# Attention and two MLP layers on one Trainium2 core: batches cut into halves of 256 queries, the first block in single precision

## The chip, the cores and the metric

One core of one Trainium2 chip runs the whole kernel. The metric is device microseconds of one execution; lower is better. TensorE (PE) multiplies, VectorE (DVE) and ScalarE (ACT) do the elementwise work and empty PSUM, GpSimd (POOL) helps where PSUM is not read, SyncE (SP) issues the DMAs.

## The reference

Three stages follow one another. Single precision comes in and goes out; the MLP weights come in double precision.

```python
# attention: batch 4, heads 8, seq 576, head_dim 64
scores = scale * np.matmul(q, k.transpose(0, 1, 3, 2))
thresh = np.max(scores, axis=-1, keepdims=True) - tau
scores = np.where(scores >= thresh, scores, -1000000000.0)
attn = np.exp(scores - np.max(scores, axis=-1, keepdims=True))
attn = attn / (np.sum(attn, axis=-1, keepdims=True) + 1e-09)
x = np.matmul(attn, v)            # -> (2304 tokens, 512)
# layer 1: 512 -> 2048 -> 512
r = np.maximum(x @ w_in, 0.0)
x = (s * (r * r) + b) @ w_out
# layer 2: 512 -> 2048 -> 512
h = x @ w_in2
out = (h * (1.0 / (1.0 + np.exp(-1.702 * h)))) @ w_out2
```

The mask is sharp (only scores within tau of the row's maximum count), so the scores are computed in single precision or better. The rest keeps that precision by splitting a number into two f16 parts, high and low, and adding three products instead of one.

## The kernel before

**A plan, not a loop.** The class `Plan` collects steps (`add`): engines with an estimated cost, what is read and written, and a due time `prio`. `run` goes through the plan once with these costs and, on each engine, always starts the ready step with the smallest due time; the order that comes out is emitted as it stands, so each engine's queue is fixed before the run. `KN` holds the due times (in us) and buffer counts. A tile pool with `bufs` buffers gives them out in the order in which the steps were added.

**Attention** goes by pairs of heads, 4 for each of 4 batches, with 9 tiles of 128 queries a pair (`attention`, `tile_step`): PE computes 128 x 576 scores into two PSUM banks (L525 for batches 0 and 1, two single-precision products of 64 rows; L518 for batches 2 and 3, from operands split before), DVE finds the negative maximum `nm` (L539), then the threshold `tb` (L544) and the exponential's bias `nb` (L550), ACT takes the exponential (L557), DVE masks and sums (L561). ACT then writes an f16 copy `p16` (L335), POOL its low part (L570, L571), and a transposing DMA on SP's queue turns both into `PT` (L573). Scores have two buffers `S`; every third of the first 53 tiles goes to a third buffer `Sx`. After a pair's last tile its sums are inverted and turned by TensorE (L608, L612), the values are multiplied in f16 in 14 terms (`finish_main`, L633; the last 64 queries in `finish_last`, L661), and the result is scaled and split into `xs`, the operand of layer 1. `scan_v` finds the largest value of each head first, since V is scaled before it is split (`prep_v`).

**Weights.** Each of layer 1's 32 weight rows (512 KB of doubles) is loaded, turned into single precision by a cast on ACT or DVE (L745) and a DVE step (L749, `convert`); each group of four rows gets a norm (`norm`: PE products L783, DVE, PE L791, DVE) and is split into f16 parts (`split_w`, L827).

**Layer 1** goes by units of 256 queries: two for each batch and a ninth for the last 64 queries of all four. A unit needs `xs` of its whole batch. Its first half is 8 pairs of 128 hidden columns (`pair`, L901, 24 f16 matmuls a pair into one PSUM bank; ACT's L908 and L909 empty it), its second half two banks (`bank`, L929). One PSUM bank (`y`) serves pairs, banks and norms until `widen` turns the two banks of `Sx` into two more (`yy`); `widen` waits for the last tile in `Sx`.

**Layer 2** (L1054, L1099) follows in blocks of 512 tokens.

PSUM's eight banks: `S` 4, `Sx` 2 (later `yy` 2), `T` 1 (turned sums, values), `y` 1.

## Time and profile before

| | |
|---|---|
| median of 3 runs | 1074.03 us (1072.44 to 1074.36) |
| the profiled execution | 1071.84 us, span 1069.7 us |
| mean granted TensorE clock | 0.943 of full speed |
| PE busy | 976.5 us (91%), 7193 matmuls |
| DVE busy | 648.8 us (61%) |
| ACT busy | 580.6 us (54%) |
| POOL busy | 259.8 us (24%) |
| DMA | 121.88 MB, mean 114 GB/s |

The profile shows one execution. A span runs from the first instruction to the last; the profiled time has 2.1 us around it. Busy shares are averages over stages that differ, so the slices and stretches are read before the averages. The granted clock is TensorE's, as a share of 2.4 GHz; it has two levels, 1.2 and 2.4 GHz, and a share between them is a mix.

### The profile page before, as it was taken

To read this page: it belongs to the slowest core of one execution; us is meant where nothing else is said; L and a number is where in the kernel's file an instruction comes from. 1 tells how busy PE (TensorE), PEld (TensorE's weight loads), DVE (VectorE), ACT (ScalarE), POOL (GpSimd) and SP (SyncE) were. 2 spreads that over 40 slices of the span, in tenths; PEclk is the share of its full clock that TensorE was granted. 3 is DMA by queue.
4 is the path that set the end of the run, shared out by engine and by line. 5 is a ranking of instruction groups with operands and counts; after the bars stand their busy time and mean duration, and the time that the engine had idled before them with its cause. 6 is when DMAs were issued, how large, how long until landed. Compare 5 with 4: busy or idle time off the path is not lost.

```text
span 1069.7 us, 19065 instructions
## 1 busy us (share of the span) xinstructions
PE 976.5 (91%) x7193; PEld 652.5 (61%) x7193; DVE 648.8 (61%) x1517; ACT 580.6 (54%) x996; POOL 259.8 (24%) x359
## 2 busy tenths in 40 slices
PE   4665667879999999999999999999999999999998
PEld 2332234547888988888888888844444444444653
DVE  7989988887876788778534367486343333223210
ACT  5676676676675777776544567374332323323311
POOL 3554443333455666455400000000000000000000
PEclk7686567979999999999999999999999999999999
DMA  8899989856678687868632356201001001000001
GB/s 230 199 200 233 248 244 212 231 116 128 133 151 143 141 174 166 166 134 155 106 99 63 116 186 225 73 1 40 20 11 59 10 10 30 21 10 10 21 1 40
DMA packets 208636, 121.88 MB, mean 114 GB/s; under 512 B 178264, under 2 KB 183456, under 8 KB 208544
## 3 DMA queue, kind: packets, MB, share of 16 engines
q1 hardware_dynamic: 208544, 120.66, 47.4%
q8 instruction: 57, 0.93, 0.4%
q14 instruction: 35, 0.29, 0.1%
HBM read 68.16 MB, written 10.00 MB: 73 GB/s over the span
## 4 chain that ended last, share of the span: by engine, by line
PE 66%; DVE 2%; ACT 1%; issue 0%; ACTq 0%; DVEq 0%
PE S L1099 17%; PE yy L1054 12%; PE yy L929 10%; PE yy L901 7%; PE y L1054 6%; PE y L901 4%; PE y L929 4%; PE S L518 3%; PE T L633 2%; PE T L661 0%; ACT e L557 0%; DVE nm L539 0%; DVE l L827 0%; ACT gt L952 0%; DVE e L561 0%
## 5 line engine op out<-in xcount | busy, mean ns | idle before, releaser
L901 PEld LDWEIGHTS <-wb 128*128 128x128 f16 x1728 | 167.7, 99 | 28.4 <-issue 6.7
L929 PEld LDWEIGHTS <-wb 128*128 128x128 f16 x1728 | 168.5, 98 | 25.6 <-issue 3.8
L570 POOL TENSOR_TENSOR p<-e,p 128x512 f16<-128x512 f32 x112 | 134.3, 1199 | 200.5 <-ACT p L335 168.8
L1054 PEld LDWEIGHTS <-l 128*128 128x128 f16 x960 | 93.9, 98 | 92.7 <-issue 0.2
L929 PE MATMUL yy<-g,wb 128*128 128x256 f16 x1248 | 144.2, 275 | 1.7 <-ACT gt L952 0.9
L1054 PE MATMUL yy<-xs,l 128*128 128x512 f16 (+1 forms) x636 | 128.4, 357 | 0.0
L557 ACT ACTIVATE e<-S,nb 128x576 f32<-128x576 f32 x127 | 92.0, 734 | 40.7 <-DVE tb L544 18.5
L561 DVE SCALAR_TENSOR_TENSOR e<-S,tb,e 128x576 f32<-128x576 f32 x127 | 101.7, 810 | 20.4 <-ACT e L557 19.4
L901 PE MATMUL yy<-xs,wb 128*128 128x256 f16 x960 | 113.0, 273 | 0.0
L539 DVE TENSOR_REDUCE nm<-S 128x1 f32<-128x576 f32 x127 | 93.6, 749 | 31.2 <-PE S L518 17.6
L1099 PE MATMUL S<-wb,g 128*128 128x512 f16 x480 | 106.7, 379 | 0.0
L901 PE MATMUL y<-xs,wb 128*128 128x256 f16 x768 | 92.6, 277 | 3.8 <-DVE n L793 1.9
L335 ACT ACTIVATE p<-e 128x576 f16<-128x576 f32 x112 | 75.5, 677 | 35.9 <-DVE e L561 14.5
L1066 DVE SCALAR_TENSOR_TENSOR gt<-gt,yy 128x512 f32<-128x512 f32 (+1 forms) x53 | 33.3, 632 | 91.9 <-ACT gt L1062 91.9
L1099 PE MATMUL S<-wb,lg 128*128 128x512 f16 x384 | 85.5, 379 | 0.0
L1099 PEld LDWEIGHTS <-g 128*128 128x128 f16 x480 | 47.0, 98 | 55.7
L337 ACT ACTIVATE gt<-S,x2y 128x512 f32<-128x512 f32 x17 | 11.7, 688 | 112.6 <-PE S L1099 112.6
L525 PE MATMUL S<-kk,qa 64*128 64x288 f32 (+1 forms) x136 | 34.3, 599 | 37.5 <-DVE e L561 15.4
L1054 PE MATMUL y<-xs,l 128*128 128x512 f16 (+1 forms) x324 | 67.9, 359 | 0.0
L1099 PEld LDWEIGHTS <-lg 128*128 128x128 f16 x384 | 37.6, 98 | 45.1
L331 DVE CAST g<-gt 128x512 f16<-128x512 f32 x43 | 21.5, 501 | 60.6 <-ACT gt L909 60.5
L1066 DVE SCALAR_TENSOR_TENSOR gt<-gt,y 128x512 f32<-128x512 f32 (+1 forms) x27 | 17.2, 637 | 63.3 <-ACT gt L1062 63.3
(171 smaller groups left out, 1461.2 us busy)
## 6 DMA issues: line engine op xcount, KB each, us to landing
wst<-in_moe_w_in SPq DMA_DIRECT2D x32, 512.0 KB, 4.1
wst<-in_moe_w_out SPq DMA_DIRECT2D x32, 512.0 KB, 4.3
rv<-in_v SPq DMA_DIRECT2D x29, 320.0 KB, 3.2
raw<-in_k SPq DMA_DIRECT2D x16, 288.0 KB, 3.4
raw<-in_q SPq DMA_DIRECT2D x16, 288.0 KB, 3.2
yd<-gt SPq DMA_DIRECT2D x18, 256.0 KB, 2.3
l<-yd SPq DMA_DIRECT2D x16, 256.0 KB, 4.4
out<-gt SPq DMA_DIRECT2D x16, 256.0 KB, 2.0
```

Of the source, the lines that this page charges most:

```text
L335: nc.scalar.activation(dst(), src(), AF.Copy)
L518: nc.tensor.matmul(Sp[:, half, :HALF], q[h][j][:, qcols[h]], k[h][:, half * HALF : (half + 1) * HALF], start=(h, j) == (heads[0][0], 0), s ...
L525: nc.tensor.matmul(Sp[to, half, :HALF], q[h][r, qcols[h]], k[r, h * HALF : (h + 1) * HALF])
L539: {"DVE": 668.0}, lambda _: nc.vector.tensor_reduce(nm.ap, Sv(), AX.XY, ALU.max, negate=True), [Sp], [nm],
L557: lambda _: nc.scalar.activation(ev(), Sv(), AF.Exp, bias=nb.ap, scale=1.0), [Sp, nb], [e],
L561: lambda _: nc.vector.scalar_tensor_tensor(ev(), Sv(), tb.ap, ev(), ALU.is_ge, ALU.mult, accum_out=p["acc"][:, i, 0:1]),
L570: nc.gpsimd.tensor_tensor(p16[:, S + H2 :], e[:, :MAIN], p16[:, :MAIN], ALU.subtract)
L901: nc.tensor.matmul(hps[:, h, :], W[:, i, j, kk * P : (kk + 1) * P], x[:, k, kk, cols], start=t == 0, stop=t == len(terms) - 1,)
L929: nc.tensor.matmul(yp[:, h, :], self.W[0, 1, c][:, i, j, i0 * P : (i0 + 1) * P], u["g"][c][:, k, j, :], start=t == 0, stop=t == len(terms) ...
L1054: nc.tensor.matmul(hps[:, :n], W[:, i, j, kk * P : (kk + 1) * P], x[:, k, kk, :], start=t == 0, stop=t == 11)
L1066: lambda _: nc.vector.scalar_tensor_tensor(gt[:, :n], gt[:, :n], 1.0, hps[:, :n], ALU.add, ALU.mult),
L1099: nc.tensor.matmul(yp(), blk["g"][f // 2][:, k, f % 2, cols], self.W[1, 1, f // CH][:, w, f % CH, :], start=n == 0, stop=n == 47,)
```

## The change

Each batch's first 512 queries are worked in two halves of 256 (`heads`): for batches 0 and 1 all four pairs of heads do the first half (4 tiles a pair), then all four the second half with the last 64 queries (5 tiles); for batches 2 and 3 each pair does both halves in turn and keeps K and Q. Layer 1's units now need only their own half (`x_of`).

Batch 0 is worked in single precision (`fa` 2 halves): the masked exponential is turned by TensorE, five turns a tile into a two-bank buffer `TP`, and copied to `PT` by ACT; V is used as it was loaded, in 5 terms instead of 14. The bias is the maximum itself, and `tb` is computed on POOL. No f16 copy, low part or transposing DMA is left for these tiles. The value maxima of batch 0 are taken along the way.

The first unit of layer 1 is worked in single precision too (`fu` 1; `pair32`, `bank32`): 4 products for each 128 hidden columns instead of 12, with weights that are converted but neither normed nor split. The norms and splits of the first weights come during this unit's pairs (`split_in`), those of the second weights after it.

The two banks that `Sx` had go to `TP` first, then (`swap`) to a third scores buffer for every third tile of batches 1 and 2 (`sx` 24 pairs), then (`widen`, due at 300) to `yy`. Only steps that use `yy` wait for `widen` now (`gate`). Attention's PE steps get due times 300 us earlier than those of the other engines (`first`). Due times are set anew; `g` buffers are no longer lent to attention; `xs` has 4 buffers of half the size, `rv` 2 and `V` 4 buffers. `bank` is cut into four steps a half instead of two, and layer 2's `xs` into two buffers.

```diff
-    "lend": 6, "lp": 3, "lV": 1, "boost": 29.63, "mix": 14, "a0": 0, "p0": 20.89, "a1": 78.55, "p1": 28.98, "a2":
-    166.74, "p2": 0.72, "a3": 221.7, "p3": 0.72, "u0": 85.49, "du": 55.73, "win": 6.56, "wout": 60.47, "cpace":
-    4.0, "w2": 436.49, "c2pace": 7.19, "t2": 622.67, "d2": 126.93, "c0": 3, "tw": 2, "cast": 1, "g": 6, "wb": 9,
-    "xs": 2, "gt": 3, "lg": 6, "l8": 5, "scan": 0, "sx": 53.0, "wide": 0.45, "x2": 39.35, "y2": 0.99, "wf": 0,
-    "wm": 1, "wl": 1, "wv": 1, "wq": 1, "nm": 1, "tb": 22.97, "sc": 0, "eb": 3, "pb": 2, "pt0": 2, "pt1": 1, "rv":
-    1, "V": 1, "parts": 8, "raw": 1, "spread": 8,
+    "first": 300.0, "lend": 0, "lp": 3, "lV": 1, "boost": 0, "mix": 14, "a0": 0, "p0": 12.0, "a1": 110.0, "p1":
+    13.0, "a2": 230.0, "p2": 32.0, "a3": 360.0, "p3": 32.0, "u0": 60.0, "d0": 28.0, "opace": 2.0, "du": 44.0,
+    "win": 2.0, "wout": 55.0, "cpace": 3.4, "w2": 360.0, "c2pace": 5.0, "t2": 622.67, "d2": 126.93, "c0": 3, "tw":
+    2, "cast": 1, "g": 6, "wb": 9, "xs": 4, "gt": 3, "lg": 6, "l8": 5, "scan": 2, "fu": 1, "fa": 2, "half": 2,
+    "a0b": 50.0, "p0b": 14.0, "a1b": 165.0, "p1b": 14.0, "si": 110.0, "sp": 7.0, "so": 150.0, "sop": 5.0, "vs0":
+    300.0, "tbp": 1, "nbs": 1, "rvk": 1, "wide": 300.0, "sx": 24, "x2": 39.35, "y2": 0.99, "wf": 0, "wm": 1, "wl":
+    2, "wv": 3, "wq": 1, "nm": 1, "tb": 22.97, "sc": 0, "eb": 3, "pb": 2, "pt0": 2, "pt1": 1, "rv": 2, "V": 4,
+    "parts": 8, "raw": 1, "spread": 8,
...
-        op["prio"] = self.prio if prio is None else prio
+        op["prio"] = (self.prio if prio is None else prio) - self.first * ("PE" in engines)
...
+        if p["first"]:
+            p["k"], p["q"] = p["first"]["k"], p["first"]["q"]
+            return
...
+        if not p["f32"] and (b, hp) in self.kept:
+            p["v"] = self.kept[b, hp]
+            return
+        rv = self.at("rv", [P, 2, KS * D], F32, KN["rv"])
         self.load(lambda: rv.ap, lambda: self.v[b, hp], [rv], P * 2 * KS * D * 4)
-        V = self.at("V", [P, 2, 2 * KS, D], F16, KN["V"], KN["lV"])
-        p["v"] = V
+        if p["f32"]:
+            p["v"] = rv
+            if p["unit"] % 2 == 0:
+                self.most(b, hp, rv)
+            return
+        V = self.at("V", [P, 2, 2 * KS, D], F16, KN["V"])
+        p["v"] = self.kept[b, hp] = V
         part = lambda i: V.ap.rearrange("p h (i x) d -> p h i (x d)", i=2)[:, :, i]
...
         k, q = p["k"], p["q"]
-        Sp = self.ps("S", [P, 2, 512], (p["b"] * NP + p["hp"]) * R + p["turn"] < KN["sx"] and p["turn"] % 3 == 2)
-        p["turn"] += 1
-        if i < 8:
-            h, t = divmod(i, 4)
+        Sp, swap = self.ps("S", [P, 2, 512]), []
+        if not p["f32"] and p["unit"] * NP + p["hp"] < KN["sx"]:
+            if self.swaps is None:
+                self.swap()
+            self.nth += 1
+            if self.nth % 3 == 0:
+                Sp, swap = Buf(self.py, "Sx", [P, 2, 512], F32, 1), self.swaps
...
-            lambda _: nc.vector.tensor_scalar(tb.ap, nm.ap, -1.0, self.under, ALU.mult, ALU.subtract), [nm], [tb],
+            {"POOL": 130.0} if p["f32"] and KN["tbp"] else {"DVE": 180.0},
+            lambda e: self.eng[e].tensor_scalar(tb.ap, nm.ap, -1.0, self.under, ALU.mult, ALU.subtract), [nm], [tb],
             prio=self.plan.prio - KN["tb"] * pace,
...
-        nb = self.at("nb", [P, 1], F32, bufs=4)
-        add(
-            {"DVE": 130.0},
-            lambda _: nc.vector.tensor_scalar(nb.ap, nm.ap, LOG_SP, None, ALU.add), [nm], [nb],
-            prio=self.plan.prio - KN["tb"] * pace - 1.0,
-        )
+        nb = nm
+        if not plain:
+            nb = self.at("nb", [P, 1], F32, bufs=4)
+            add(
+                {"DVE": 130.0},
+                lambda _: nc.vector.tensor_scalar(nb.ap, nm.ap, LOG_SP, None, ALU.add), [nm], [nb],
+                prio=self.plan.prio - KN["tb"] * pace - 1.0,
+            )
...
         )
+        if p["f32"]:
+            Tp = Buf(self.px, "TP", [P, 2, 512], F32, 1)
+
+            def turn(_):
+                for j in range(KS):
+                    n = min(P, S - j * P)
+                    nc.tensor.transpose(Tp[:n, j // 4, j % 4 * P : (j % 4 + 1) * P], e[:, j * P : j * P + n], self.ident)
+            add({"PE": (KS * 110.0, 60.0)}, turn, [e], [Tp])
+            for w, (rows, j) in enumerate(((P, slice(0, 4)), (H2, slice(4, 5)))):
+                self.copy(
+                    lambda rows=rows, j=j: pt()[:rows, j],
+                    lambda rows=rows, w=w: Tp[:rows, w, : (4, 1)[w] * P].rearrange("p (j q) -> p j q", q=P),
+                    [Tp], [(PT, (part, w))], (4, 1)[w] * P, psum=True,
+                )
...
-        add(
-            {"DVE": dve(512, psum=True) + 126},
-            lambda _: nc.vector.scalar_tensor_tensor(x.ap, Up.ap, vb[:, 20 + hp : 21 + hp], x.ap, ALU.mult, ALU.mult),
+        xs = self.x_of(p["unit"])
+        if p["unit"] < KN["fu"]:
+            add(
...
+    def heads(self, b, starts, paces):
+        two, apart = ((0, 256, False), (256, 256, True)), b < KN["half"]
+        if apart:
+            order = [(w, hp, starts[w] + hp * paces[w], paces[w]) for w in range(2) for hp in range(NP)]
+        else:
+            order = [
+                (w, hp, starts[0] + paces[0] * (hp + w * 4 / R), paces[0] * (4 + w) / R) for hp in range(NP) for w in range(2)
+            ]
+        pairs = []
+        for w, hp, start, pace in order:
+            q0, n, last = two[w]
+            pairs.append({
+                "f32": 2 * b + w < KN["fa"], "unit": 2 * b + w, "b": b, "hp": hp, "q0": q0, "n": n, "last": last, "T": n // P,
+                "count": 2 * (n // P) + last, "start": start, "pace": pace, "apart": apart,
...
+    def gate(self, bank):
+
+        return self.changes if bank.pool is self.pw else []
...
+    def pair32(self, u, jp):
+
+        nc, add = self.nc, self.plan.add
+        x, n = self.x_of(u["n"]), 256
+        hps = self.bank_of([P, 2, n])
+        c = 2 * jp // CH
+        W = self.stage[0, 0, c]
+        for h in range(2):
+            j = (2 * jp + h) % CH
+
+            def mm(_, h=h, j=j):
+                for kk in range(KD):
+                    nc.tensor.matmul(
+                        hps[:, h, :], W[:, j, kk * P : (kk + 1) * P], x[:, kk, :], start=kk == 0, stop=kk == KD - 1
+                    )
+            add(
+                {"PE": (KD * 430.0, 60.0 * h)}, mm,
+                [(W, j), x] + self.gate(hps), [(hps, h)],
+            )
+        gt = Buf(self.wp, "gt", [P, 512], F32, KN["gt"])
+        flat = lambda: hps.ap.rearrange("p a b -> p (a b)")
...
+    def bank32(self, u, ib):
+
+        nc, add, n = self.nc, self.plan.add, 256
+        yp = self.bank_of([P, 2, n])
+        ev = Buf(self.wp, "gt", [P, 2, n], F32, KN["gt"])
+        for h in range(2):
+            i0 = 2 * ib + h
+            for c in range(NCH):
+                def mm(_, h=h, i0=i0, c=c):
+                    for j in range(CH):
+                        nc.tensor.matmul(
+                            yp[:, h, :], self.stage[0, 1, c][:, j, i0 * P : (i0 + 1) * P], u["g"][c][:, j, :],
+                            start=(c, j) == (0, 0), stop=(c, j) == (NCH - 1, CH - 1),
+                        )
+                add(
+                    {"PE": (CH * 430.0, 60.0 * (c == NCH - 1))}, mm,
+                    [(self.stage[0, 1, c], j) for j in range(CH)] + [u["g"][c]] + self.gate(yp) + [(yp, 0)] * h, [(yp, h)],
+                )
+        flat = lambda t: t.ap.rearrange("p a b -> p (a b)")
+        self.copy(lambda: flat(ev), lambda: flat(yp), [yp], [ev], 512, psum=True, also=0)
+        yd, cols = self.yd[u["b"]], slice(u["at"], u["at"] + n)
...
+        def split_in(c):
+            stage = self.stage[0, 0, c]
+            self.norm(0, 0, c, stage)
+            self.scale_in(0, c, stage)
         F = DFF // P
         for m, which, t, pace in (
-            (0, 0, KN["win"], KN["cpace"]), (0, 1, KN["wout"], KN["cpace"]),
+            (0, 0, KN["win"], KN["cpace"]), (0, 1, KN["wout"], KN["opace"]),
             (1, 0, KN["w2"], KN["c2pace"]), (1, 1, KN["w2"] + F * KN["c2pace"], KN["c2pace"]),
         ):
...
-        t, d, wend = KN["u0"], KN["du"], KN["wout"] + F * KN["cpace"]
-        at(t + 2 * d * KN["wide"] - 0.01, self.widen)
-        for u in units:
+        units = [{"n": i, "b": i // 2, "at": i % 2 * 256, "g": []} for i in range(2 * B + 1)]
+        t, d = KN["u0"], KN["d0"]
+        plain = units[: KN["fu"]]
+        for u in plain:
+            for jp in range(F // 2):
+                at(t + d * jp * 2 / F, self.pair32, u, jp)
+                if u is plain[-1] and 2 * jp % CH == CH - 2:
+                    at(t + d * jp * 2 / F + 0.01, split_in, 2 * jp // CH)
+            for ib in range(2):
+                at(t + d + d * ib / 2, self.bank32, u, ib)
+            t += 2 * d
+        for c in range(NCH):
+            at(t - 0.1, lambda c: self.norm(0, 1, c, self.stage[0, 1, c]), c)
+        at(t - 0.09, lambda: self.scale_out(0, [self.stage[0, 1, c] for c in range(NCH)]))
+        d = KN["du"]
+        at(KN["wide"], self.widen)
+        for u in units[len(plain) :]:
             if u["b"] == B:
                 at(t - 10.0, self.load_x)
             for jp in range(F // 2):
                 at(t + d * jp * 2 / F, self.pair, u, jp)
+            if u is units[len(plain)]:
+                at(t + d - 0.01, self.bias)
             for ib in range(2):
-                at(max(t + d, wend) + d * ib / 2, self.bank, u, ib)
-            t = max(t + d, wend)
+                at(t + d + d * ib / 2, self.bank, u, ib)
+            t += d
         t, d = KN["t2"], KN["d2"]
         for k, b in enumerate((0, 1, 2, 3, B)):
             n = MAIN if b < B else B * H2
...
+    def swap(self):
+
+        def change(_):
+            self.pxs.close()
+            self.py.pool = self.pxs.enter_context(self.tc.tile_pool(name="py", bufs=1, space=PSUM))
+        self.swaps = [Buf(None, "swap", None, None)]
+        self.after(self.px, self.plan.add({"SP": 1.0}, change, [], self.swaps))
...
-        op = self.plan.add({"SP": 1.0}, change, [], self.changes)
-        for b in self.plan.bufs:
-            if b.pool is self.px:
-                for steps in b.log.values():
-                    op["after"].update(*steps)
+        op = self.plan.add({"SP": 1.0}, change, self.swaps or [], self.changes)
```

## Rows read from the trace of the kernel before

**Rows 1.** Page, part 2: busy share and granted clock in 40 slices, in tenths.
```profile
PE   4665667879999999999999999999999999999998
PEclk7686567979999999999999999999999999999999
```

**Rows 2.** Stretches: us; busy us PE, PEld, DVE, ACT, POOL; clock, DMA, GB/s.
```profile
0.00:222.00 222.00, 138.09 (x964) 77.64 (x966) 195.98 (x517) 149.08 (x243) 98.24 (x139) 0.74 0.91 224
222.00:691.00 469.00, 464.21 (x4401) 395.48 (x4398) 320.38 (x758) 304.70 (x544) 161.51 (x220) 0.99 0.61 137
691.00:1069.70 378.70, 374.15 (x1834) 179.40 (x1832) 132.46 (x243) 126.79 (x210) 0.00 (x0) 1.00 0.06 21
```

**Rows 3.** First and last start of layer 1's matmuls, by line.
```profile
L901 PE MATMUL y<-xs,wb x768: 269/273/421, 173.5 to 666.9; 128*128 128x256 f16 x192
L929 PE MATMUL yy<-g,wb x1248: 269/273/421, 223.4 to 690.9; 128*128 128x256 f16 x179
```

**Rows 4.** DVE groups, 0 to 107 us: count, busy us, mean ns, idle before.
```profile
L539 DVE TENSOR_REDUCE nm<-S 128x1 f32<-128x576 f32 x24 | 17.8, 743 | 6.0 <-PE S L525 6.0
L561 DVE SCALAR_TENSOR_TENSOR e<-S,tb,e 128x576 f32<-128x576 f32 x22 | 17.7, 807 | 1.9 <-ACT e L557 1.9
L561 DVE DVE_READ_ACCUMULATOR e<-S,tb,e 128x1 f32 x22 | 1.8, 81 | 0.0
L749 DVE SCALAR_TENSOR_TENSOR wb<-wst,tw 128x512 int32<-128x512 int32 x11 | 10.8, 990 | 0.0
L544 DVE TENSOR_SCALAR tb<-nm,under 128x1 f32<-128x1 f32 x34 | 6.7, 201 | 0.0
L550 DVE TENSOR_SCALAR nb<-nm 128x1 f32<-128x1 f32 x34 | 4.9, 143 | 0.1
```

**Rows 5.** PE timeline: start us, us, line, operation, count, idle before.
```profile
193.15 3.21 PE L633 MATMUL T<-PT,g 128*64 128x512 f16 x28
206.10 2.78 PE L901 MATMUL y<-xs,wb 128*128 128x256 f16 x24 [0.79 <-ACT gt L908]
230.80 0.60 PE L608 MATMUL T<-ident,ri 128*64 128x128 f32 x4
244.97 2.79 PE L901 MATMUL y<-xs,wb 128*128 128x256 f16 x24
247.70 0.76 PE L525 MATMUL S<-kk,qb 64*128 64x288 f32 x4
248.45 2.78 PE L901 MATMUL y<-xs,wb 128*128 128x256 f16 x24
```

**Rows 6.** PE's groups, 0 to 222 us.
```profile
L525 PE MATMUL S<-kk,qa 64*128 64x288 f32 (+1 forms) x124 | 31.9, 606 | 37.5 <-DVE e L561 15.4 <-issue 10.3 <-ACT kk L387 8.5
L901 PE MATMUL y<-xs,wb 128*128 128x256 f16 x144 | 19.2, 297 | 3.8 <-DVE n L793 1.9 <-DVE nb L550 1.1 <-ACT gt L908 0.8
L633 PE MATMUL T<-PT,g 128*64 128x512 f16 x84 | 13.9, 501 | 0.5 <-ACT rm L617 0.5
```

**Rows 7.** Ns (min/median/max) of turn weights; of scores from 187 us.
```profile
L612 PEld LDWEIGHTS T<-ident,ri x8: 133/133/183, 43.2 to 279.2; 128*128 128x128 f32 x8
L525 PE MATMUL S<-kk,qb x40: 402/428/507, 187.9 to 263.6; 64*128 64x288 f32 x32, 64*64 64x288 f32 x8
L525 PEld LDWEIGHTS S<-kk,qb x40: 129/183/186, 187.9 to 263.4; 64*128 64x128 f32 x32, 64*64 64x64 f32 x8
```

**Rows 8.** ACT's pass that frees a layer-1 bank, whole run.
```profile
L908 ACT ACTIVATE gt<-y 128x512 f32<-128x512 f32 x32 | 18.9, 591 | 13.4 <-PE y L901 13.0 <-DMA yd<-gt 0.2
```

**Rows 9.** Stretches as in rows 2.
```profile
107.00:133.70 26.70, 16.04 (x66) 7.90 (x68) 25.94 (x78) 16.59 (x25) 13.07 (x19) 0.56 1.01 248
187.00:213.80 26.80, 22.66 (x223) 15.68 (x221) 22.41 (x50) 18.59 (x31) 8.90 (x12) 1.00 0.81 231
```

**Rows 10.** Exponentials in 320 to 426 us; maxima of the whole run.
```profile
L557 ACT ACTIVATE e<-S,nb x29: 719/733/746, 322.2 to 421.4; 128x576 f32<-128x576 f32 x29
L539 DVE TENSOR_REDUCE nm<-S x127: 696/751/759, 9.9 to 521.6; 128x1 f32<-128x576 f32 x127
```

More of the change, by code (lines that the diff above doesn't have):

```diff
@@ L383, in prep_qk @@
             for h, q in enumerate(p["q"]):
-                self.load(lambda q=q: q.ap, lambda h=h: self.q[b, hp, :, h], [q], P * S * 4)
+                c = slice(0 if h and p["last"] else p["q0"] + h * H2, S if p["last"] else p["q0"] + h * H2 + p["n"])
+                if not p["apart"]:
+                    c = slice(0, S)
+                self.load(
+                    lambda q=q, c=c: q[:, c], lambda h=h, c=c: self.q[b, hp, :, h, c], [q], P * (c.stop - c.start) * 4
+                )
             add(
@@ L530, in tile_step @@
         else:
-            used, cost = [k] + [q[h] for h, _ in heads], pe(1, HALF, True) + 370.0
-        add({"PE": (cost, 60.0)}, scores, used, [Sp])
+            used, cost = [k] + [q[h] for h, _ in heads], pe(1, HALF, True) + 60.0
+        add({"PE": (cost, 60.0)}, scores, used + swap, [Sp])
         Sv = lambda: Sp[:, :, :HALF]
@@ L535, in tile_step @@
         tb = self.at("tb", [P, 1], F32, bufs=4)
-        pace = p["pace"] / R
+        pace, plain = p["pace"] / p["count"], p["f32"] and KN["nbs"]
         add(
@@ L711, in attention @@
             do(step, pairs[-1], R)
-    def heads(self, b, start, pace):
-        return [
-            {
-                "turn": 0, "b": b, "hp": hp, "start": start + hp * pace, "pace": pace,
+        for b in range(B):
+            if b not in self.vb:
+                self.scan_v({"b": b, "hp": 0, "unit": 2 * B - 2})
+    def heads(self, b, starts, paces):
[12 more added lines that the diff above has]
+                "count": 2 * (n // P) + last, "start": start, "pace": pace, "apart": apart,
+                "first": pairs[-1] if w and not apart else None,
                 "parts": b * NP + hp >= KN["parts"], "spread": b * NP + hp >= KN["spread"],
-            }
-            for hp in range(NP)
-        ]
+            })
+        return pairs
     def split(self, hi, lo, src, reads, writes, cols, **kw):
@@ L1167, in mlp, with after @@
             fn(*a)
+    def swap(self):
[4 more added lines that the diff above has]
+        self.after(self.px, self.plan.add({"SP": 1.0}, change, [], self.swaps))
+    def after(self, pool, op):
+        for b in self.plan.bufs:
+            if b.pool is pool:
+                for steps in b.log.values():
+                    op["after"].update(*steps)
     def widen(self):
@@ L1211, in run @@
             self.lp = Later()
-            self.attention(sum((self.heads(b, KN["a%d" % b] * 1e3 - boost * 1e3, KN["p%d" % b] * 1e3) for b in range(B)), []))
-            self.late = Buf(None, "late", None, None)
+            plan.first = KN["first"] * 1e3
+            of = lambda k, b: [1e3 * KN[k + "%d%s" % (b, x)] for x in ("", "b")[: 1 + (b < KN["half"])]]
+            self.attention(sum((self.heads(b, [a - boost * 1e3 for a in of("a", b)], of("p", b)) for b in range(B)), []))
+            self.late, plan.first = Buf(None, "late", None, None), 0.0
             def change(_):
```

256 lines of the change are left out of this document (152 added, 104 removed).

## The prediction

> **What bounds the kernel now.** I read the page's slices first, then stretches of the span, then groups and timelines inside them. The slices [rows 1] show two kernels in one: up to about slice 8 TensorE is busy 40 to 80% of the time at a granted clock of 0.5 to 0.8, afterwards it is full at full clock. The stretches put numbers to it [rows 2]: in the first 222 us PE is busy 138 us at clock 0.74 while DVE is busy 196 us; from 222 to 691 us (the rest of attention, and layer 1) PE is busy 99%; the last 379 us are layer 2, also 99%. So from 222 us on only the amount of TensorE work counts, and before that DVE sets the pace. The first matmul of layer 1 starts at 173.5 us and its second half at 223.4 us [rows 3]. Why so late: DVE needs 0.74 + 0.81 us per tile of 128 queries for maximum and mask, 0.20 + 0.14 us for the two small steps and 0.08 us for reading the sum (about 2.0 us), and 0.99 us per weight row in this stretch; by 107 us it has done 34 of batch 0's 36 tiles (by the count of `tb`) and 11 of layer 1's 32 weight rows [rows 4]. So the time is the moment from which PE has its hands full, and the work left then.
>
> **The change part by part.** The sum goes by one moment, t*: when the changed kernel has done as much TensorE work as the kernel before had at 222 us, its own extra work included. From there both have the same work left, which took 1069.7 - 222 = 848 us.
>
> (1) Prices at full clock, from start to next start [rows 5]: a scores tile 0.75 us (247.70 to 248.45); 24 matmuls of 256 columns in f16 2.73 us (244.97 to 247.70), 0.114 each; 28 value matmuls 3.2 us; four small turns by TensorE 0.60 us with the pipe's end, 0.11 to 0.15 each.
>
> (2) TensorE work done before 222 us [rows 6] (the x124 row is the first of four of its line, 288 matmuls in all, four to a tile's worth): 72 x 0.75 = 54, 168 value matmuls = 6 x 3.2 = 19, 144 matmuls of layer 1 = 16, and some 21 for the turned sums (54 x 0.13 = 7) and for norms, short value products and little things, some 20 steps of under 1 us: 110 us.
>
> (3) Work added, all of it to batch 0 and the first block. A single-precision matmul shows as two instructions (a tile has four for two products). One of 288 columns takes 402 ns at full clock [rows 7], of which some 160 ns is the pipe's end (273 ns for a matmul that issues each 114 ns), so 0.24 us, or 0.213 us for 256 columns. The first block has 128 such products: 128 x 2 x 0.213 = 55 us against 384 x 0.114 = 44 us in f16: +11. Values of batch 0: 8 x 5 x 2 x 0.213 = 17 against 4 x 3.2 = 13: +4. Turning the probabilities: five a tile; no row has a turn with a fresh 128-column weight in sequence, so between 0.11 us (the turns above; L612's weights load in 0.13) and 0.19 us (the longer load of a score's weights) [rows 5, 7]. I take 0.15, nearer the row of the same operation: 36 x 5 x 0.15 = 27 (20 to 34). Sum 42 us (35 to 50). The rows thus give a turn about half the time of a 128-column product (two instructions, 0.21 us). The Trainium skill ("TensorE: Matmul & The Clock Gate", Terms) has the transpose mode four times faster for single precision: by it a turn would be 0.05 us, an estimate from that page, and the sum 17 us lower. The turns of these rows do not show that, so it is not used. The short products of the last 64 queries change by under 1 us.
>
> (4) Work removed is not TensorE's. For the 36 tiles of batch 0 the f16 copy on ACT, POOL's low part, and the transposing DMAs on SP's queue go; in their place ACT empties the turned tile (128x512 from PSUM like L908's 0.59 us [rows 8], plus a quarter of that). DVE loses 0.14 us a tile (the bias is the maximum itself) and 0.20 us (`tb` on POOL, hidden beside the 0.73 us exponential [rows 10]; if POOL takes longer, the mask waits for the rest). DVE's tile falls from 2.0 to 1.64 us. K is loaded and scaled a second time for two batches' halves: 8 ACT copies and 2.3 MB, beside other work. One wait is added: the first scores tile in the third buffer waits until ACT has emptied the last turned tile, whose banks it takes; matmuls of layer 1 stand behind it on PE. It comes two tiles after, so I cost it at nothing, and at about one ACT pass (0.6 us) if ACT is behind.
>
> (5) When the first block can start, T0. It needs 16 tiles, not 36, and no norm and no split of weights. DVE: 16 x 1.64 = 26, 16 weight rows 13 to 16, four value maxima 3, sums and products 4, casts and constants 4: 52 us. Its first maximum starts near 10 us, and over the first 222 us DVE was busy for 196, some 0.91 of the rest [rows 2], so T0 = 10 + 52/0.91 = 67 (60 to 80). The transfers are 12 MB (16 rows of 512 KB, and 3.5 MB of heads); the first 222 us carried 224 GB/s with transposes among them [rows 2], by which they take 54 us: no bound if the queue keeps its order.
>
> (6) From T0 to t*. Done by T0: 16 tiles (0.75 + 0.75), values 4 x 2.1, turned sums 2: 35 us. Left: 110 + 42 - 35 = 117 us. In that stretch DVE has about 73 us (20 tiles 33, 16 rows 14, 16 splits like rows 14, norms and sums 12), ACT about 74 (20 tiles at 0.73 + 0.59 + 0.15 make 29, three passes in each of the block's 8 pairs 15, casts and splits like passes of 0.6 to 0.7 some 23, K and sums 7), so all three engines are well loaded, and the norms go through one bank with DVE between their steps. PE's share was 0.85 (22.66 of 26.80) in the nearest stretch, with one bank of layer 1 and DVE full, and 0.99 once it is ahead [rows 2, 9]. I take 0.88, near the first: 117/0.88 = 133, t* = 200 (187 to 230).
>
> (7) After t*. The third scores buffer is now kept until batch 2's scores are done, near 400 us, so layer 1 has one PSUM bank until then instead of three from 223 us. A pair cannot start before ACT's 0.59 us pass of the last has freed the bank. Where a scores tile stands between two pairs this costs nothing (244.97, 247.70 and 248.45 follow without a gap, all pairs of the one bank [rows 5]), and there are about two tiles to a pair. Bounds 0 and 0.15 x 200 = 30 us; I take 8, near the row without a gap. Sum: 200 + 848 + 8 = 1056 us of span. The profiled execution took 1071.84 for its span of 1069.7 (2.1 outside), and the median of the runs is 2.2 above it: 1056 + 4.3 = about 1060 against 1074.03.
>
> **The rivals.** *Dense at once*: PE is full from T0, 117/0.97 = 121, t* = 188, no loss to the bank: 1036 + 4 = 1040. For it: a scores tile fills the bank's gap; against: all three engines are loaded at the same time.
>
> *Attention becomes the bound* (slower): with priority over everything, batches 2 and 3 went at 29 tiles in 106 us, 3.65 us a tile, and the last maximum was at 521.6 us [rows 10]; PE still had 160 us of layer 1 then, a reserve. Now batch 1 starts only after batch 0's 36 tiles and the weights, at 135 to 165 us instead of 108, and its tiles have due times up to 488 us behind older work of layer 1 on DVE and ACT. After the last tile PE must still do units 6 to 8 (3 x 44) and layer 2 (379), less some 10 us by which unit 6 is early: end = last tile + 501. At 3.65 us the last of 108 tiles comes at 529 to 559: 1030 to 1060, no bound. It decides from 569 us on, that is from 3.9 us a tile with a start at 150; at 4.0 us: 582 + 501 + 4 = 1087.
>
> *The single-precision stage runs late*: if weight rows come as slowly as before (11 in 107 us [rows 4]), or ACT's passes hold it up, T0 moves to 85 or the share to 0.75; or the clock stays low: while PE had only scores and turns, the granted clock was 0.56 [rows 9], mostly the lower level of 1.2 GHz, and the turns of batch 0's second half could keep it there. Then t* = 223 to 230, end 225 + 848 + 8 + 4 = 1085. Even is at t* = 214. That the change does not do what it says is this case. Against it: half of the work between T0 and t* is plain products of the block, back to back.
>
> *The one bank holds layer 1 back*: where no tile stood between two pairs PE waited 0.79 us for ACT (206.1 us [rows 5]). If the tiles come in bunches, the upper bound of (7) is paid: 30 us, and t* slips to 208 for the same reason: 1090. Even is at a loss of 22 us. The Trainium skill ("Perfetto Trace Analysis", Optimization Strategy) says of such a repeating gap on the engine that should be full that it can mean too few buffers; the trace agrees for that one gap, and shows none where tiles stand between.
>
> **How the numbers follow.** Forecast 0.45 (own range 1047 to 1073), dense 0.18, attention late 0.17, stage late 0.13, one bank 0.07. The predicted time is 1060; eight times in ten between 1034 and 1092. A measurement tells about 0.2% (2 us) from no change: faster 0.60 (dense, and most of the forecast), same 0.08 (the forecast's upper edge), slower 0.32 (the last three, less their lower edges).
>
> **What would show it.** Right: the first single-precision matmul of layer 1 at 60 to 80 us; PE's slices at 8 or 9 from slice 3 on with clock 9; about 40 us more busy PE; layer 1's other banks (`yy`) only near 400 us; last maximum at 530 to 560 us. Wrong: PE slices of 6 or 7 past 200 us (bank or ACT), holes between 400 us and the last tile with PE waiting for `xs` (attention), clock at 5 to 6 between 70 and 150 us, or turns far over 0.19 us.

## The result and the profile after

The changed kernel takes 1079.82 us (median of 4 runs, 1078.88 to 1082.31) against 1073.36 (1072.44 to 1074.36): 1.0064 times the kernel before, 95% interval 1.0043 to 1.0084. It is slower by 0.6%, where 1060 was forecast. The profiled execution took 1078.88 us with a span of 1077.1.

The page (engine, busy us, share, instructions; then busy share and granted clock in 40 slices, in tenths), and stretches with the columns of [rows 2]:

```profile
PE 1010.1 (94%) x7605; PEld 689.8 (64%) x7605; DVE 644.5 (60%) x1500; ACT 584.9 (54%) x1057; POOL 212.6 (20%) x337
PE   4799999899998999999999999699999999999998
PEclk9999999998999999999999999999999999999999
```

```profile
67.00:190.00 123.00, 118.85 (x839) 85.38 (x838) 102.27 (x268) 93.87 (x180) 31.24 (x56) 1.00 0.70 180
190.00:251.00 61.00, 52.97 (x581) 39.10 (x579) 50.49 (x125) 46.34 (x83) 26.66 (x37) 0.92 0.57 113
190.00:685.00 495.00, 466.69 (x4658) 397.68 (x4657) 352.69 (x867) 317.68 (x580) 173.00 (x249) 0.99 0.60 135
685.00:702.00 17.00, 8.09 (x27) 2.84 (x26) 15.66 (x35) 13.03 (x21) 0.00 (x0) 0.79 0.05 17
685.00:1077.10 392.10, 378.52 (x1832) 179.93 (x1830) 138.63 (x256) 129.66 (x214) 0.00 (x0) 0.99 0.07 23
```

Against [rows 1], the slow start is gone: slices 3 to 9 stand at 8 and 9 and the clock is high from the first slice on. But the middle is no longer full (PE is busy 466.69 of 495 us, where [rows 2] had 464.21 of 469), and there is a notch: the 26th slice is a 6, and in the 17 us from 685 PE works 8.09 at clock 0.79. Groups of the whole run by line, with durations (min/median/max) and first and last start:

```profile
L1017 PE MATMUL y<-xs,wb x128: 379/379/483, 66.3 to 142.5; 128*128 128x256 f32 x128
L1049 PE MATMUL y<-g,wb x128: 379/379/483, 147.5 to 190.5; 128*128 128x256 f32 x128
L990 PE MATMUL yy<-xs,wb x456: 269/273/283, 420.6 to 662.1; 128*128 128x256 f16 x152
L1077 PE MATMUL yy<-g,wb x768: 269/273/283, 432.4 to 684.7; 128*128 128x256 f16 x192
L570 DVE TENSOR_REDUCE nm<-S x120: 717/751/759, 9.6 to 541.8; 128x1 f32<-128x576 f32 x120
L1203 PE MATMUL yy<-xs,l x636: 272/379/631, 687.0 to 1051.4; 128*128 128x512 f16 x126, 128*128 128x256 f16 x33
```

Layer 1 starts at 66.3 us (L1017; before 173.5 [rows 3]), its last matmul at 684.7 instead of 690.9: 6.2 us gained. The rest of the span takes 392.3 us from there (1077.1 - 684.8) instead of 378.7: 13.6 us lost. The sum is the 7.4 us by which the span grew. So the first question is what happened to layer 2, whose arithmetic the change doesn't touch. PE and DVE there, in order of time (start, us, line, operation, count, idle before):

```profile
684.99 0.30 PE L1159 MATMUL yy<-ident,x2t 128*128 128x128 f32 x1
687.00 0.38 PE L1203 MATMUL yy<-xs,l 128*128 128x512 f16 x1 [1.71 <-ACT xs L339]
688.51 2.29 PE L1203 MATMUL yy<-xs,l 128*128 128x512 f16 x5 [1.13 <-DVE xs L1187]
698.28 0.59 PE L1203 MATMUL yy<-xs,l 128*128 128x512 f16 x1 [4.50 <-ACT xs L339]
700.44 2.29 PE L1203 MATMUL yy<-xs,l 128*128 128x512 f16 x5 [1.57 <-DVE xs L1187]
```

```profile
687.71 1.41 DVE L1187 SCALAR_TENSOR_TENSOR xs<-l,x2t,xs 128x512 f16<-128x512 f32 x2
689.03 10.68 DVE L917 SCALAR_TENSOR_TENSOR wb<-wb,o 128x512 f16<-128x512 f32 x16
699.63 1.41 DVE L1187 SCALAR_TENSOR_TENSOR xs<-l,x2t,xs 128x512 f16<-128x512 f32 x2
```

and ACT there:

```profile
687.71 9.91 ACT L339 ACTIVATE wb<-wb,o 128x512 f16<-128x512 f32 x16
697.52 1.32 ACT L339 ACTIVATE xs<-l,x2t 128x512 f16<-128x512 f32 x2
```

Two things stand in the wrong order. A split is two passes, the high part on ACT (L339) and the low part on DVE (L917), and the 16 splits of layer 2's second weights stand on both engines (9.91 and 10.68 us) between the two halves of the first block's x, which has its high part from ACT and its low part from DVE (L1187). PE's wait of 4.50 us ends with ACT's part of the second half, the 1.57 us behind it with DVE's. On PE, the turn of that block's maximum (L1159), from which x is scaled, comes behind layer 1's last product; in the kernel before (L1011 there) it came at 669.6, 21 us ahead of that end, and x was ready when layer 1 ended:

```profile
669.61 0.27 PE L1011 MATMUL yy<-ident,x2t 128*128 128x128 f32 x1
674.54 2.73 DVE L1038 SCALAR_TENSOR_TENSOR xs<-l,x2t,xs 128x512 f16<-128x512 f32 x4
```

Both are due times. The change moves `w2` and `c2pace` from 436.49 and 7.19 to 360 and 5.0, so the last weights and their splits are due near 515 instead of 659, and layer 1's last second half from 587 to 468; the first block's x stayed at 622.67 - 39.35 = 583, which was ahead of both and is now behind both.

In the middle, from 190 to 685 us, PE idles 28.3 us (4.8 in the kernel before from 222 to 691). The longest of ACT's waits from 200 to 545 us, and of PE's from 190 to 545 (us in total, times, longest):

```profile
ACT e L590 <- POOL p L619: 19.4, 17, 2.0
ACT p L337 <- DMA PT<-p: 17.2, 18, 2.0
```

```profile
PE y L990 <- ACT gt L997: 8.0, 12, 1.2
PE S L549 <- DVE e L594: 2.4, 4, 0.8
PE y L1077 <- ACT gt L1100: 2.0, 4, 0.7
PE y L990 <- ACT gt L1100: 2.0, 3, 0.7
PE y L1077 <- ACT gt L997: 1.5, 3, 0.7
```

ACT waits for POOL and the transposing DMA to give back `e` and `p16`; PE waits 13.5 us for the one bank (the four lines with `y`).

### The profile page after: what moved, and what is told of

Its sections match the earlier page's. It is cut to its first block, busy times and chain, and to the rows that moved or that the text cites. A ratio compares the mean times of both kernels' runs of the same rounds, so it can differ in the third digit from the quotient of the medians.

```text
span 1077.1 us, 19797 instructions
## 1 busy us (share of the span) xinstructions
PE 1010.1 (94%) x7605; PEld 689.8 (64%) x7605; DVE 644.5 (60%) x1500; ACT 584.9 (54%) x1057; POOL 212.6 (20%) x337
## 4 chain that ended last, share of the span: by engine, by line
PE 49%; DVE 5%; DMA 3%; ACT 2%; issue 1%; POOL 0%; SPq 0%; POOLq 0%; DVEq 0%; ACTq 0%
PE S L1248 17%; PE yy L1203 11%; PE y L1203 6%; PE yy L1077 5%; PE yy L990 3%; PE y L990 3%; DMA wst<-in_moe_w_out 2%; PE y L1077 1%; DVE wb L917 1%; DMA PT<-p 1%; PE S L549 1%; PE T L689 1%; DVE wb L835 0%; DVE l L917 0%; ACT e L590 0%
## 5 line engine op out<-in xcount | busy, mean ns | idle before, releaser
L990 PEld LDWEIGHTS <-wb 128*128 128x128 f16 x1536 | 148.3, 98 | 34.0 <-issue 14.6
L1077 PEld LDWEIGHTS <-wb 128*128 128x128 f16 x1536 | 148.4, 98 | 29.6 <-issue 11.2
L990 PE MATMUL y<-xs,wb 128*128 128x256 f16 x1080 | 131.3, 275 | 10.3 <-ACT gt L997 8.0
L594 DVE SCALAR_TENSOR_TENSOR e<-S,tb,e 128x576 f32<-128x576 f32 x120 | 96.8, 812 | 27.5 <-ACT e L590 22.9
L570 DVE TENSOR_REDUCE nm<-S 128x1 f32<-128x576 f32 x120 | 88.6, 751 | 22.7 <-PE S L556 13.4
L1077 PE MATMUL y<-g,wb 128*128 128x256 f16 x768 | 90.1, 273 | 3.6 <-ACT gt L1100 2.0
L1077 PE MATMUL yy<-g,wb 128*128 128x256 f16 x768 | 87.8, 273 | 3.5 <-ACT gt L1100 2.3
L1215 DVE SCALAR_TENSOR_TENSOR gt<-gt,yy 128x512 f32<-128x512 f32 (+1 forms) x53 | 33.4, 631 | 95.8 <-ACT gt L1211 95.8
L590 ACT ACTIVATE e<-S,nb 128x576 f32<-128x576 f32 x84 | 61.0, 734 | 32.8 <-POOL p L619 17.5
L339 ACT ACTIVATE gt<-S,x2y 128x512 f32<-128x512 f32 x17 | 11.7, 688 | 119.7 <-PE S L1248 119.7
L1211 ACT ACTIVATE gt<-yy,x2h 128x512 f32<-128x512 f32 (+1 forms) x53 | 33.9, 642 | 42.5 <-PE yy L1203 38.1
L990 PE MATMUL yy<-xs,wb 128*128 128x256 f16 x456 | 52.4, 273 | 0.0
L352 DVE TENSOR_TENSOR g<-gt,g 128x512 f16<-128x512 f32 x61 | 49.1, 808 | 4.2 <-ACT g L337 3.4
```

Of the source, the lines that this page charges most:

```text
L352: engines, lambda e: self.eng[e].tensor_tensor(dst(), a(), b(), ALU.subtract), reads, writes, **kw
L570: {"DVE": 668.0}, lambda _: nc.vector.tensor_reduce(nm.ap, Sv(), AX.XY, ALU.max, negate=True), [Sp], [nm],
L590: lambda _: nc.scalar.activation(ev(), Sv(), AF.Exp, bias=nb.ap, scale=1.0), [Sp, nb], [e],
L594: lambda _: nc.vector.scalar_tensor_tensor(ev(), Sv(), tb.ap, ev(), ALU.is_ge, ALU.mult, accum_out=p["acc"][:, i, 0:1]),
L990: nc.tensor.matmul(hps[:, h, :], W[:, i, j, kk * P : (kk + 1) * P], x[:, k, kk, :], start=t == 0, stop=t == len(terms) - 1,)
L1077: nc.tensor.matmul(yp[:, h, :], self.W[0, 1, c][:, i, j, i0 * P : (i0 + 1) * P], u["g"][c][:, k, j, :], start=t == 0, stop=t == len(terms) ...
```

## The experiments

All compute the whole reference; times are medians, ratios are to the kernel before on the same chip, with their 95% intervals.

| run | edit | us | ratio |
|---|---|---|---|
| e1_splitlate | splits of layer 2's second weights due at t2 + 10 | 1072.52 | 0.9983 (0.9965 to 1.0001) |
| e2_sx16 | third scores buffer for batch 1 only, then banks | 1093.8 | 1.0170 (1.0147 to 1.0193) |
| e3_sx0 | no third scores buffer | 1098.41 | 1.0217 (1.0172 to 1.0261) |
| e4_halves_f16 | halves without single precision | 1106.17 | 1.0294 (1.0252 to 1.0336) |
| e5_three_p16 | e1, third `p16` buffer | 1065.04 | 0.9907 (0.9886 to 0.9928) |
| e6_due_earlier | e1, batches 2 and 3 due earlier | 1069.82 | 0.9955 (0.9937 to 0.9973) |
| e7_no_first | e1, PE's due times as the others' | 1192.79 | 1.1102 (1.1085 to 1.1118) |
| e8_lend | e1, `g` buffers lent to batch 1 | 1125.95 | 1.0489 (1.0460 to 1.0518) |
| e9_before_p16 | kernel before, third `p16` buffer | 1073.97 | 0.9999 (0.9988 to 1.0010) |
| e10_p16_only | change, third `p16` buffer | 1070.92 | 0.9966 (0.9948 to 0.9985) |
| e11_p16_due | e5, due times of e6 | 1063.48 | 0.9900 (0.9877 to 0.9923) |
| e12_p16_due_e4 | e11, fourth `e` buffer | 1064.13 | 0.9907 (0.9884 to 0.9931) |
| e13_x2_first | change, first block's x due earlier | 1073.75 | 1.0009 (0.9990 to 1.0028) |
| e14_x2_p16 | e5, x of e13 | 1063.37 | 0.9909 (0.9878 to 0.9939) |
| e15_x2_p16_due | e11, x of e13 | 1063.22 | 0.9912 (0.9889 to 0.9934) |
| e16_x2_splits | change, x of e13, splits due at t2 + 45 | 1065.67 | 0.9933 (0.9906 to 0.9959) |
| e17_all | e15, splits due at t2 + 45 | 1055.13 | 0.9839 (0.9815 to 0.9863) |

### Layer 2's start: e1, e13, e16

```diff
-            if m and f == DFF // P - 1 and which:
-                self.scale_out(m, [self.stage[m, 1, c] for c in range(NCH)])
...
+        at(KN["t2"] + 10.0, lambda: self.scale_out(1, [self.stage[1, 1, c] for c in range(NCH)]))
```

> The changed kernel with one step moved: the splits of layer 2's second weights (16 DVE steps of 0.67 us, which stood in DVE's queue between the second and third part of the first block's x) get a due time behind that x. Theory 1 (the hole): PE idles some 9 us of the 17 us after layer 1's end only because of these steps; then the hole is under 4 us and the time falls by 9 to 14 us, to 1066 to 1071. Rival: the first block waits for something else there (its loads, the scale of the block, the weights of the second half), the hole moves behind the first block and the time stays at 1077 to 1081.

1072.52: 7.3 us under the changed kernel, a little short of what was expected, and the 4.50 us wait is gone. But layer 2 still took 384.8 us (1067.5 - 682.7), and PE still waited 1.71 and 1.13 us for `xs`. What was left could be the same cause in PE's queue, so e13 moves x alone:

```diff
-            at(t - KN["x2"], self.load_x2, blk)
+            at(t - (KN["x2"] if k else 130.0), self.load_x2, blk)
```

> The changed kernel with one due time moved: the first block's x of layer 2 is due 130 us ahead of t2 (492.67) instead of 39.35 (583.32); its steps then stand ahead of the splits on DVE, and TensorE's turn of its maximum (L1159) stands between layer 1's last banks instead of behind them, as in the kernel before. If the whole 13.6 us that layer 2 takes more is this order: layer 2 in 379 to 381 us, no hole behind layer 1, and 1079.8 - 13 = 1066 to 1068, some 5 us under e1. If only the splits matter: as e1, 1071 to 1074, with the waits for xs of 1.7 and 1.1 us left at layer 2's start.

The forecast of 1066 to 1068 missed: 1073.75. The turn stood inside layer 1's banks and x came in time, but the 16 splits now stood ahead of DVE's pass that frees layer 2's banks (L1215), and on ACT ahead of the pass that feeds it (L1211), and the wait had only changed its name (PE's and DVE's timelines of e13):

```profile
682.80 1.46 PE L1203 MATMUL y<-xs,l 128*128 128x512 f16 x6
697.21 4.03 PE L1203 MATMUL yy<-xs,l 128*128 128x512 f16 x12 [6.48 <-DVE gt L1215]
686.55 10.01 DVE L917 SCALAR_TENSOR_TENSOR wb<-wb,o 128x512 f16<-128x512 f32 x15
```

So either DVE is short of time there, or both orders must be put right at once, with the splits spread out (due at t2 + 45, one to four at a time between the block's passes):

> e13's early x for the first block of layer 2, and the 16 splits due inside that block (t2 + 45), where they stand one to three at a time between the block's other passes on DVE; nothing else of the changed kernel is touched. In e13 the x came in time but PE then waited 6.5 us for DVE's pass L1215 behind the same 16 splits. If the order of these two on DVE is all of layer 2's 13.6 us: layer 2 in 378 to 381 us, no wait over 1 us from 680 to 702, and 1079.8 - 13 = 1066 to 1069. If DVE is short there whatever the order: layer 2 at 385 us or more, 1071 to 1075 as e1 and e13.

1065.67, 14.2 us under the changed kernel. Its DVE and PE, and the stretch of its layer 2:

```profile
683.50 2.74 DVE L1187 SCALAR_TENSOR_TENSOR xs<-l,x2t,xs 128x512 f16<-128x512 f32 x4 [1.53 <-ACT xs L339]
691.21 2.73 DVE L917 SCALAR_TENSOR_TENSOR wb<-wb,o 128x512 f16<-128x512 f32 x4
693.86 0.68 DVE L1215 SCALAR_TENSOR_TENSOR gt<-gt,yy 128x512 f32<-128x512 f32 x1
694.46 0.74 DVE L917 SCALAR_TENSOR_TENSOR wb<-wb,o 128x512 f16<-128x512 f32 x1
695.12 0.68 DVE L1215 SCALAR_TENSOR_TENSOR gt<-gt,y 128x512 f32<-128x512 f32 x1
```

```profile
686.98 0.36 PE L858 MATMUL yy<-fro,ones 128*128 128x4 f32 x2
687.46 1.45 PE L1203 MATMUL y<-xs,l 128*128 128x512 f16 x6
688.75 2.75 PE L1203 MATMUL yy<-xs,l 128*128 128x512 f16 x12
```

```profile
686.90:1065.90 379.00, 374.24 (x1833) 179.35 (x1832) 134.36 (x248) 126.27 (x210) 0.00 (x0) 1.00 0.07 24
```

Layer 2 takes 379.0 us, as in the kernel before (378.7). That shows the 13.6 us to be the order of x and the splits, nothing else: due times alone, no work.

### Attention's buffers: e5, e9, e10, e6, e11, e12

e5 and e6 stand on e1; the first is `"pb": 2` to `3`, the second

```diff
-    13.0, "a2": 230.0, "p2": 32.0, "a3": 360.0, "p3": 32.0, "u0": 60.0, "d0": 28.0, "opace": 2.0, "du": 44.0,
+    13.0, "a2": 225.0, "p2": 16.0, "a3": 290.0, "p3": 16.0, "u0": 60.0, "d0": 28.0, "opace": 2.0, "du": 44.0,
```

> The kernel of e1 with three instead of two buffers for p16. In the changed kernel ACT waits 17 us between 200 and 545 us for a p16 buffer (for the transposing DMA to have read it). Theory 4 (attention's buffers hold the stretch back): that wait goes, the last maximum moves from 540 us to 530 or earlier, PE's idle time between 190 and 545 us falls from 25 to under 19 us, and the time falls by 3 to 8 us from e1, to 1064 to 1069. Rival (the one bank of layer 1): PE's holes there are waits for the bank, attention is not late; within 2 us of e1.

1065.04, 7.5 us under e1; the last maximum came at 532.9 instead of 540.1. The two waits of ACT shown above, in the same stretch of e5:

```profile
ACT e L590 <- POOL p L619: 3.6, 5, 1.0
ACT p L337 <- DMA PT<-p: 3.2, 3, 1.9
```

36.6 us of ACT's waits (35.9 in e1) have become 6.8, both kinds by the one buffer. PE's idle time from 190 to 545 fell by less than expected, from 25.4 us in the changed kernel (25.0 in e1) to 23.5 (331.49 busy of 355), so most of the gain lies inside its busy time: 3435 matmuls stand in that stretch instead of 3373 (3390 in e1). The control is the same edit to the kernel before, where ACT waited 13.9 us for the transposes too:

> The kernel before with a third p16 buffer (pb 2 -> 3), nothing else. Theory 4 (the buffer pays only because the halves' attention is one of the two things that pace layer 1): in the kernel before the last maximum came about 160 us ahead of layer 1's end and PE idled 4.8 us from 222 to 691, so the time stays within 2 us of before's 1073.4. Rival: the third buffer shortens any attention of this kernel that stands over layer 1, so before falls too, by 4 to 9 us, to 1064 to 1069, and the halves are then worth nothing.

No change (0.9999). The wait went here too (13.9 to 0.9 us from 200 to 545), but the last maximum came no earlier (529.6, before 521.6): other waits took its place. So less of this wait brought nothing here; that the buffer pays only where attention paces layer 1 fits this control and is not shown further. And alone, on the changed kernel:

> The changed kernel with a third p16 buffer alone; the splits of layer 2's weights stay ahead of the first block's x. If the two causes (the splits' order, the missing buffer) add: 1079.8 less the 7.5 us that the buffer brought in e5 over e1 = about 1072 (1070 to 1075), last maximum at 530 to 535, layer 1's end at 677 to 680 and the hole of 10 to 12 us behind it. If layer 1's earlier end only leaves PE to wait longer for the same splits (their time is set by DVE's queue, not by layer 1): 1077 to 1080, with a hole wider than 12 us.

1070.92, 8.9 us gained, layer 1's last product at 677.3, with the hole behind it as before: the two causes add.

> The kernel of e1 with the tiles of batches 2 and 3 due earlier (from 225 and 290 us, 16 us a pair, instead of 230 and 360 us, 32 us a pair). Theory 5 (due times hold attention back on DVE and ACT): the last maximum moves from 540 to 525 us or earlier and the time falls by 3 us or more from e1. Rival (buffers set attention's pace, or layer 1's passes then come later and the one bank is held longer): the last maximum moves by under 6 us, the time is within 3 us of e1 or above it.

1069.82, some 2.7 us under e1 (the intervals overlap), with the last maximum at 534.0. On top of the buffer the same due times brought 1.6 us (e11), within what a measurement can tell, though the last maximum came at 527.8; a fourth `e` buffer brought nothing (e12):

> e5 (splits late, third p16 buffer) with the due times of batches 2 and 3 earlier (225 and 290, their parts 16 us apart, for 230 and 360, 32 us apart). If due times still leave DVE and ACT short of attention before 420 us: the last maximum at 515 to 525 and 1059 to 1063. If attention now runs at the pace of its own engines: within 2 us of e5's 1065.0, last maximum 528 to 536.

> e11 with a fourth e buffer (eb 3 -> 4). If ACT's exponentials still wait for e buffers behind POOL and DVE: last maximum 5 to 10 us earlier than e11's and 2 to 4 us less. If not (in e5 only 3.6 us of ACT's waits from 200 to 545 were for that): within 2 us of e11.

### The bank for layer 1: e2, e3

The bank waits are the price of the kept scores buffer. e2 is `"wide": 200.0, "sx": 16`, e3 `"wide": 150.0, "sx": 0`:

> The changed kernel with the third scores buffer for batch 1 only, so that layer 1's other two banks come after batch 1's scores (near 290 us instead of 420). Theory 2 (one bank): between 204 and 420 us PE idles 20 us, most of it waiting for ACT to empty the one bank; about 10 of them come back: 1067 to 1073. Rival (attention): with two scores buffers batch 2 goes slower, the last maximum moves from 542 us to 555 or later, and the time stays within 3 us of 1080 or rises.

> The changed kernel with no third scores buffer after the turned tiles of batch 0; layer 1's other two banks come at about 150 us. Theory 2 (one bank): nearly all of the 20 us come back: 1058 to 1066, and PE waits for ACT's passes of layer 1 for under 3 us between 204 and 420 us. Rival (attention): two scores buffers for batches 1 and 2 hold attention up, the last maximum is 20 us later, and the time is 1078 or more.

Both lose, 14.0 and 18.6 us against the change, although layer 1 had its banks at 302.7 us (e2) and near 251 (e3) instead of 420.6. The last maximum moves from 541.8 to 557.3 and 564.0, and PE runs out of work at the end of attention; e2, then the changed kernel:

```profile
500.00:550.00 50.00, 39.23 (x380) 33.31 (x377) 32.07 (x87) 28.41 (x48) 21.51 (x32) 0.87 0.60 118
```

```profile
500.00:550.00 50.00, 48.31 (x481) 42.16 (x481) 33.79 (x86) 33.62 (x60) 23.09 (x30) 1.00 0.60 113
```

So the 13.5 us of waits for the bank buy more than they cost. What one bank costs by itself was not tried: every other owner of a bank is attention.

### What single precision is worth: e4

`"fu": 0, "fa": 0, "u0": 90.0`, the first weights normed and split as they are converted:

> The changed kernel with its halves but without any single precision: batch 0 and the first block of layer 1 in f16 as in the kernel before, first block due at 90 instead of 60 us. It leaves out the 42 us of extra TensorE work. Theory 3 (the early start pays): layer 1 cannot start before about 100 us, the granted clock is low until then, and the time is 8 to 20 us above the changed kernel: 1088 to 1100. Rival (the extra work eats the early start): within 4 us of 1080, or below.

1106.17, above what either side expected: halves, banks and due times alone cost some 32 us against before (2.94%), and the single-precision start gives 26 of them back. Some 11 of the 32 are the order at layer 2's start again (390.0 us of layer 2 for 378.7), and the other due times of e4 are still those set for the single-precision start, so 26 us is the price of taking it away from this plan, not from any plan. Without it the start is the old one; e4's first 200 us:

```profile
0.00:100.00 100.00, 52.29 (x311) 30.64 (x311) 85.96 (x224) 62.66 (x101) 31.57 (x50) 0.78 0.95 262
100.00:200.00 100.00, 75.21 (x757) 51.20 (x755) 77.38 (x211) 72.92 (x128) 45.63 (x61) 0.81 0.76 174
```

### PE's priority and the lent buffers: e7, e8

On e1, `"first": 0.0` and `"lend": 8`:

> The kernel of e1 with attention's PE steps due at the same time as its other steps, not 300 us earlier. Theory 6 (the priority is what fills the gaps of the one bank): without it attention falls behind, the last maximum comes after 552 us and the time rises by 5 to 20 us. Rival (the order on PE hardly matters, since PE is full either way): within 3 us of e1.

> The kernel of e1 with layer 1's g buffers lent to attention for p16 of batch 1, as the kernel before did for its first six pairs. Theory 4 (attention's buffers): batch 1's tiles come faster, its last maximum some 10 us earlier, and the time falls by 1 to 5 us. Rival: the lent buffers are missing in layer 1, whose units wait for g; the time is the same or 2 to 10 us above e1.

e7: 1192.79, 120 us over e1, far more than either side expected. The last maximum came at 648.7, and PE starved behind attention, at a clock to match:

```profile
545.00:685.00 140.00, 92.43 (x744) 75.17 (x745) 89.24 (x233) 66.64 (x109) 59.33 (x88) 0.77 0.53 109
```

Its waits there are for single passes (12.4 us for ACT's `qb`, 12.3 for DVE's masks, 10.9 for `nb`). That layer 1's matmuls, now due first, make attention's short steps late one after another would fit this, but was not tested apart. e8: 1125.95, 53 us over e1, also far more than expected; the first f16 pair of layer 1 started at 308.4 us instead of 204.9. The edit lends the `g` buffers that this pair's unit needs to attention; the trace does not name the buffer.

### All that helped: e14, e15, e17

> e5 (splits late, third p16 buffer) with the same due time. If the turn of the maximum behind layer 1's last bank is what is left of the hole (layer 2 takes 386.5 us in e5, 378.7 before): 1059 to 1061, layer 2 in 379 to 381 us. If not: within 2 us of e5's 1065.0.

> e11 (e5 with batches 2 and 3 due earlier) with the same due time: by the first theory 1057 to 1060, by the second within 2 us of e11's 1063.5.

> e15 (third p16 buffer, batches 2 and 3 due earlier, early x) with the splits due at t2 + 45 too. By the first theory of e16: 1063.2 - 5 = 1056 to 1059, layer 2 in 378 to 381 us. By the second: within 2 us of e15's 1063.2.

e14 and e15 (1063.37, 1063.22) gained nothing clear, for e13's reason: DVE's L1215 behind the splits (PE waited 4.03 us for it in e14, 3.70 in e15). With the splits spread out too, e17 takes 1055.13 (1053.97 to 1056.19), 1.6% under the kernel before and 2.3% under the changed one; its layer 2 takes 379.0 us.

## Why the prediction was wrong, step by step

The direction was wrong: slower by 0.6%, where faster had 0.60. The time lies in the range (1034 to 1092), not in the forecast's own (1047 to 1073). The steps, in the prediction's numbers:

**(1) to (3), prices and added work: right.** Five turns take 0.64 us from start to next start, 0.13 each, and 28.8 us busy over all 180 (27 forecast):

```profile
70.31 0.71 PE L605 MATMUL TP<-ident,e 128*128 128x128 f32 x5
70.95 0.76 PE L556 MATMUL S<-kk,qa 64*128 64x288 f32 x4
```

The block's products go at 0.22 us (24 in 5.37, 150.31 to 155.68) where 0.213 was taken. The Trainium skill ("TensorE: Matmul & The Clock Gate", Terms) has this mode four times faster for single precision, by the estimate in the prediction 0.05 us; the trace does not agree: 0.13. It does not show whether these turns ran in that mode.

**(5) T0: right**, 66.3 us for 67.

**(6) mis-sized, to the pessimistic side.** PE's share was 0.97 (118.85 of 123 us from 67 to 190), not 0.88, the *dense at once* rival's number. The reason against it, that all three engines are loaded at the same time, was no reason: DVE was busy 102.27 us of these 123 and ACT 93.87, and PE idled 4.15 us in all. t* can be estimated from the work left at 190 us, counted in the trace by the prices of the kernel before: 240 layer-1 matmuls fewer than before at 222 (26 us); against that 48 scores matmuls more (some 7), the second weights' norms (some 5), half a pair of values, and short value products and turned sums (some 5 together). That is 9 us less, and t* near 181, not 200: 19 us better, give or take a few.

**(7) mis-sized the other way.** From t* to layer 1's end went 685 - 181 - 469 = 35 us, not 8. Of these, 23.5 are idle PE (28.3 us, less the 4.8 that the kernel before idled from 222 to 691 too): 13.5 us of waits for the bank (forecast 8) and many short ones for masks, norms and values. The other 11 or 12 lie inside the busy time and are not attributed; the mean clock does not account for them, since it is 0.99 in both stretches. The prediction priced the bank and nothing else of this stretch, as if attention ran beside layer 1 for nothing until it is late. e10 shows that it does not: a third `p16` buffer brings 8.9 us, with the last tile far from the 569 us of the *attention* rival (541.8, and 532.1 in e10). How the 8.9 us divide between idle time, clock and short breaks inside the busy time stays open; from 190 to 251 us the granted clock was 0.92 in the changed kernel, 0.94 in e1, and 1.00 with the buffer in e5 and e10.

**Layer 2: the step that failed.** "From there both have the same work left, which took 848 us" took layer 2 over unchanged. The work was the same, its order was not: `w2`, `c2pace` and layer 1's due times moved and the first block's x did not, 13.6 us. The diff showed it and the plan's rule (smallest due time first) was in the description; the comparison of the due times, 515 and 468 against 583, was not made. The prediction does not speak of `w2` and `c2pace` at all; the due times of weights set the order on DVE, ACT and PE, not only that of transfers.

The sum: 1056 - 19 + 27 + 13.6 = 1077.6 against a span of 1077.1. Steps (6) and (7) erred by similar amounts in opposite directions; that they nearly cancel is luck. With layer 2's order mended and nothing else, e16 takes 1065.67, faster than before and inside the forecast's own range; the missing `p16` buffer of (7) would have been enough to turn the sign too (e10, 1070.92), by less.

**The rivals.** *Dense at once* held for the stage it names. *Stage late* fell (slices 8 to 9 from slice 3, clock 0.97 and 1.00); the row that it leaned on for the clock, 107 to 133.7 us, held a norm's 16 products as well, not only scores and turns. *One bank* was paid at 13.5 us of waits, below its 22. None described what decided.

**What would show it.** Four marks came as written (L1017 at 66.3; `yy` at 420.6; last maximum at 541.8; busy PE up by 33.6 us, where 40 was said). The fifth, slices of 8 or 9 from slice 3 on, failed in one place, the 6 in slice 26, which is layer 2's start. The sign of being wrong that it meets (6 or 7 past 200 us) was written for the bank or ACT in layer 1: no mark was written for layer 2.

## What to carry to other kernels

When due times or priorities move, compare the order of every pair of steps that meet in one queue, also in stages whose arithmetic is untouched; write for each queue what stands at the seam of two stages. A wait at such a seam can go from one queue to the next (e1, e13) until all of them are put right (e16). A buffer that brings nothing in one kernel (e9) can be worth 8 us in the next (e5, e10).
